# Block products in place of a plain channel product: seven instead of eight, in six of eight batches

## The chip, the cores and the metric

The kernel runs on one core of one Trainium2 chip. The metric is device time in microseconds from start to end of one execution. A core has five engines that run their own instruction queues in order: TensorE (PE in the profile, its weight loads PEld), VectorE (DVE), ScalarE (ACT), GpSimd (POOL) and SyncE (SP, which only issues DMAs here). They wait for one another by semaphores.

## What is computed

```python
# attention over 8 batches, 8 heads, 576 positions, head size 64
q_d, k_d, v_d = (t.reshape(B, H, S // 4, 4, D).mean(axis=3) for t in (q, k, v))
out_up = np.repeat(sm_attn(q_d, k_d, v_d), 4, axis=2)
mask = np.abs(pos[:, None] - pos[None, :]) < 4
out_local = softmax(where(mask, scale * q @ k.T, -1e9)) @ v
x = (out_up + out_local) laid out as (8, 576, 512)
# token mixing and channel mixing
h = relu(x.T @ w_tok1) @ w_tok2          # 576 -> 256 -> 576
u = x + h.T
out = u + relu(u @ w_ch1) @ w_ch2        # 512 -> 1536 -> 512
```

## The kernel before, in words

**Main products.** Per batch, `u` (512 channels by 576 positions, channels on partitions in four blocks c) is cut along the positions into chunk 0 (256 columns) and chunk 1 (320). A chunk goes through two *channel products*. The first (`first`, L720, matmuls `c<-uh,CW` recorded at L117) makes 12 blocks f of 128 hidden channels; the second (`second`, L744, matmuls `c<-h,CX`) makes four blocks of 128 outputs from the 12. Every factor is kept as an fp16 high part and an fp16 low part, and every product is three matmuls (`PASSES`: high by high, high by low, low by high). So each product of a chunk is 144 matmuls of 128 x 128 weights on 256 or 320 columns, and each has its own weight load.

In a batch they follow one another in four stages, named A, B, C and D from here on: **A** first product of chunk 0, **B** second product of chunk 0, **C** first product of chunk 1, **D** second product of chunk 1.

**What goes with them.** Before A and C the chunk's scale is found: a maximum per partition, a transpose and a broadcast by PE (`um_t`, `um_b`), three small DVE operations (L121 to L123). Then `scaled` (L640 on) makes `uh`: ACT writes the high part (L653), DVE the low part (L655), once per block c. After each block f, `first_up` takes the result out of PSUM: ACT the high part with the ReLU (L739), DVE the low part (L741). After each output block, `second_up` adds on DVE (L767) and SP sends it out. Three PSUM banks (`m`) serve these products in turn.

**Side work.** While batch b is in its channel products, the attention and the token mixing of batch b+1 are emitted between them: `pool_q` (sums `qd` of four positions, DVE L436 and L438), `pooled` (scores `sd`, softmax `pd`, transposes `td`, product `ad` on the shortened sequence), `local` (banded scores `sc` for five tiles of positions, softmax in a buffer `P`, transposes `pT`, product `av`, result `x`) and `mix` (splits `xh`, L584 and L586; products `t1` and `t2`). `ORDER` sets how the steps of `pooled` (p0 to p3) and `local` (l0 to l4) alternate. After each piece of main work `tick` emits side work until its estimated PE time has reached `SIDE * done / (FR * 24 * S)`: `FR` is the share of the batch's main work by which the side work is to be out. The `qk` tiles of batch b+2 are loaded when the last banded scores, `sc` of tile l4, have read those of b+1; `vr` loads pass through the `w` buffers and are summed on POOL (L414, L415).

For batch 0 and the beginning of batch 1 the order comes from a planner (`drive`). From batch 1 on the program is emitted in the loop at the end, and a scheduler then places each engine's instructions; what it chose is read from the order of the built program.

## Time and profile before

| | us |
|---|---|
| median of three runs | 952.71 |
| lowest and highest | 950.33, 953.01 |
| profiled execution, whole time | 951.0 |
| its span, first to last instruction | 949.2 |

The prediction shows the lines themselves. How to read them: a group row gives busy time, the mean duration of one instruction in ns, and the idle time in front; a timeline row gives start, length, engine, line, operation and how many instructions were merged; a windows row gives busy us and number of instructions of each engine in a stretch of time. Matmuls overlap in the array, so the length of one (217 ns and more) is not the distance between two: for a merged row of n matmuls the distance is (length of the row - length of one) / (n - 1).

### The profile page before, as it was taken

Reading aid. Unit: us, or ns where it says so; the run is one execution under the profiler, and the core shown is the slowest. Engines: PE = TensorE matmul, PEld = TensorE weight load, DVE = VectorE, ACT = ScalarE, POOL = GpSimd, SP = SyncE. Lnnn points to the kernel's source line nnn. Section 1 sums busy time; section 2 is a strip of 40 time slices with the busy share of each in tenths; the row PEclk is TensorE's granted clock in tenths of the full one; section 3 lists DMA queues with packets and bytes.
Section 4 is the critical chain, followed back from the end, with each engine's and each line's share of the span. In section 5 each row is a group of like instructions: output and inputs, shape, how many; then the busy total and the mean of one; then the engine's idle time right before and its main releaser. Section 6 shows DMA issues by size and latency. Waiting matters only on the chain.

```text
span 949.2 us, 25828 instructions
## 1 busy us (share of the span) xinstructions
PE 897.8 (95%) x11420; PEld 709.8 (75%) x11427; DVE 501.1 (53%) x1191; ACT 298.1 (31%) x627; POOL 137.6 (14%) x207
## 2 busy tenths in 40 slices
PE   8578799999989999999999999999999999999998
PEld 4345677777867788677987788777887878777876
DVE  7699998337552375526652275524653275324221
ACT  2356544214232141423323142422414142322120
POOL 6476420021120002100040002200021000000000
PEclk9879999999999999999999999999999999999999
DMA  9765420430170004400062002600052000000000
GB/s 236 232 230 172 132 70 15 147 91 27 45 191 15 21 10 135 114 8 22 2 202 46 16 15 84 166 8 22 3 183 65 15 16 13 27 1 28 13 12 28
DMA packets 28223, 68.31 MB, mean 72 GB/s; under 512 B 3504, under 2 KB 14000, under 8 KB 26864
## 3 DMA queue, kind: packets, MB, share of 16 engines
q1 hardware_dynamic: 25552, 64.30, 23.1%
q10 hardware_dynamic: 2560, 2.36, 0.9%
q8 instruction: 90, 1.47, 0.7%
q14 instruction: 21, 0.17, 0.1%
HBM read 54.85 MB, written 9.44 MB: 68 GB/s over the span
## 4 chain that ended last, share of the span: by engine, by line
PE 75%; DVE 12%; DMA 6%; ACT 3%; issue 3%; POOL 0%; SPq 0%; ACTq 0%; DVEq 0%; POOLq 0%
PE c L117 50%; PE t L117 10%; PE ad L477 3%; DMA qk<-in_qk_dram 3%; DMA vw<-od 3%; PE av L545 2%; PE sc L509 2%; PE t L609 2%; PE sd L450 2%; PE td L468 1%; PE pT L532 1%; DVE uh L655 1%; ACT x L550 1%; DVE pd L458 1%; PE busy L154 1%
## 5 line engine op out<-in xcount | busy, mean ns | idle before, releaser
L117 PE MATMUL c<-uh,CW 128*128 128x256 f16 (+1 forms) x2304 | 306.1, 287 | 3.7 <-DVE h L741 2.0
L117 PE MATMUL c<-h,CX 128*128 128x256 f16 (+1 forms) x2304 | 305.7, 287 | 0.0
L117 PEld LDWEIGHTS <-CW 128*128 128x128 f16 x2304 | 218.7, 98 | 70.6 <-issue 16.7
L117 PEld LDWEIGHTS <-CX 128*128 128x128 f16 x2304 | 218.5, 98 | 58.1 <-issue 1.6
L741 DVE SCALAR_TENSOR_TENSOR h<-c,h 128x256 f16<-128x256 f32 (+1 forms) x192 | 86.7, 452 | 133.5 <-ACT h L739 133.4
L739 ACT ACTIVATE h<-c 128x256 f16<-128x256 f32 (+1 forms) x192 | 77.8, 407 | 180.8 <-PE c L117 180.5
L414 POOL TENSOR_TENSOR vr<-vr 72x256 f32<-72x256 f32 x64 | 49.9, 783 | 491.1 <-DMA vr<-in_vr_dram 491.0
L767 DVE SCALAR_TENSOR_TENSOR u<-c,io,u 128x256 f32<-128x256 f32 (+1 forms) x64 | 32.9, 514 | 102.9 <-PE c L117 102.7
L117 PE MATMUL t<-xh,W 128*128 128x512 f32 x240 | 69.0, 421 | 5.3 <-DVE xh L586 4.0
L636 DVE TENSOR_REDUCE umx<-t 128x1 f32<-128x256 f32 (+1 forms) x64 | 29.2, 457 | 84.3 <-ACT u L634 75.4
L634 ACT COPY u<-t 128x256 f32<-128x256 f32 (+1 forms) x64 | 25.5, 398 | 136.7 <-PE t L117 110.8
L117 PE MATMUL t<-W,hid 128*128 128x256 f32 (+1 forms) x384 | 67.0, 308 | 0.1
L550 ACT COPY x<-av 128x512 f32<-128x512 f32 x32 | 18.7, 583 | 121.2 <-PE c L117 52.2
L117 PEld LDWEIGHTS t<-xh,W 128*128 128x128 f32 x240 | 43.6, 192 | 16.2 <-DVE xh L586 5.3
L117 PEld LDWEIGHTS t<-W,hid 128*128 128x128 f32 x384 | 53.3, 189 | 0.6 <-DVE C_n_m L558 0.3
L545 PE MATMUL av<-vw,pt 47*32 47x64 f32 x2304 | 33.8, 231 | 11.8 <-DMA vw<-od 5.9
L545 PEld LDWEIGHTS av<-vw,pt 47*32 47x32 f32 x2304 | 27.8, 109 | 19.6 <-DVE P L516 6.3
L477 PE MATMUL ad<-vd,ptd 72*72 72x65 f32 x512 | 38.7, 228 | 1.6 <-issue 1.1
L477 PEld LDWEIGHTS ad<-vd,ptd 72*72 72x72 f32 x512 | 37.0, 145 | 2.9 <-issue 2.3
L436 DVE TENSOR_REDUCE qd<-qk 128x72 f32<-128x288 f32 x64 | 25.9, 445 | 24.5 <-DMA qk<-in_qk_dram 24.4
L653 ACT ACTIVATE uh<-u,us 128x256 f16<-128x256 f32 (+1 forms) x64 | 29.5, 524 | 26.5 <-DVE us L123 19.3
L415 POOL TENSOR_TENSOR vd<-vr 72x128 f32<-72x128 f32 x64 | 34.6, 546 | 4.0
(114 smaller groups left out, 878.7 us busy)
## 6 DMA issues: line engine op xcount, KB each, us to landing
qk<-in_qk_dram SPq DMA_DIRECT2D x32, 579.0 KB
vw<-in_vw_dram SPq DMA_DIRECT2D x32, 351.0 KB
vr<-in_vr_dram SPq DMA_DIRECT2D x64, 144.0 KB
C_raw<-in_c_dram SPq DMA_DIRECT2D x16, 512.0 KB
out_dram<-u SPq DMA_DIRECT2D x32, 160.0 KB
C_raws<-in_c_dram SPq DMA_DIRECT2D x8, 512.0 KB
out_dram<-u SPq DMA_DIRECT2D x32, 128.0 KB
vw<-od ACTq DMA_DIRECT2D x32, 72.0 KB
```

What stands on the lines that cost most here:

```text
L117: nc.tensor.matmul(ps, lhs(a), rhs(c), start=first and i == 0, stop=last and i == 2, **kw)
L414: nc.gpsimd.tensor_add(t[:, 0:2], t[:, 0:2], t[:, 2:4])
L415: nc.gpsimd.tensor_add(st.vd[:, g, 2 * pr:2 * pr + 2, :D], t[:, 0].rearrange("p (h d) -> p h d", d=D), t[:, 1].rearrange("p (h d) -> p h d ...
L436: nc.vector.tensor_reduce(o, q[:, h], axis=AX.X, op=ALU.add)
L477: nc.tensor.matmul(ps[:, g, par], pt[:, par, kg, G * g:G * g + G], st.vd[:, kg, 2 * pr + par], start=kg == 0, stop=kg == 1)
L545: nc.tensor.matmul(ps[QB * j:QB * j + QB, par, D * hp:D * hp + D], pt[p, hp, QB * j:QB * j + QB], st.vw[h][p, g, D * hp:D * hp + D], start ...
L550: nc.scalar.copy(x[:n].rearrange("p hp two d -> p two hp d"), ps[:n, :, :4 * D].rearrange("p two (hp d) -> p two hp d", hp=4))
L636: nc.vector.tensor_reduce(umx[ch][:, c:c + 1], ps, axis=AX.X, op=ALU.max, apply_absolute_value=True)
L653: nc.scalar.activation(t[:, 0], st.u[ch][c], AF.Copy, scale=s)
L739: nc.scalar.activation(ht[:, 0], ps, AF.Relu)
L741: nc.vector.scalar_tensor_tensor(ht[:, 1], ps, 0.0, ht[:, 0], ALU.max, ALU.subtract)
L767: nc.vector.scalar_tensor_tensor(us[c], banks[c], io, us[c], ALU.mult, ALU.add)
```

## The change

From batch 2 on, the first channel product of a chunk is computed as one level of Strassen's scheme (in Winograd's form). The weights of a group of three pairs of blocks (f, f+2) are seen as 2 x 2 blocks A11, A12, A21, A22, and `u` as B11, B12, B21, B22: halves of the channels by halves of the chunk's columns. `seven` makes seven block products per group instead of eight, in two groups per chunk, each product 18 matmuls on 128 or 160 columns, in three PSUM banks X, Y and Z. Partial sums are copied to SBUF by ACT (`kept`) and added by DVE; the ReLU split (`put`) works on three blocks at once.

The sums of B blocks (T1 to T4) and the seven splits per chunk are made by `combined`, which is advanced between the pieces of the second product before. The sums of weight blocks S1 to S4 are made once, during batch 1 (`weight_sums`, `last_sums`), on DVE and POOL in turn, with ACT for the high parts.

To find room: `u` and `uh` in fewer and larger tiles, `x` in 4 buffers instead of 5, one tile for the last 64 positions instead of two, `w` in 3 slots instead of 4, and from batch 2 on two `P` buffers for the banded softmax instead of three. `ORDER` is changed in its last line: the scores of tile l4 come together with the product of l2 instead of l0. `FR` is 0.78 instead of 0.9.

```diff
-FR = 0.9
+FR = 0.78
...
 ORDER = """p0+p1 p0 p1 p0 p1 l0+l1 l0 l1 p0 p0 p1 p1 l0 l1 l0 l1 p0 p0 p1 p1 l0 l0 l1 l1
 p2+p3 p2 p3 p2 p3 l2+l3 l2 l3 p2 p2 p3 p3 l2 l3 l2 l3 p2 p2 p3 p3 p3
-l0+l4 l0 l4 l2 l2 l4 l4 l1+l2 l1 l2 l3 l3 l4 l4 l3+l4 l3 l4"""
+l0+l1 l0 l1 l2 l2 l3 l3 l2+l4 l2 l4 l4 l4 l4 l4 l3+l4 l3 l4"""
+FIRSTS = (0, 1, 4, 5, 8, 9)
+BY_GROUP = (0, 1, 4, 2, 3, 6, 5, 8, 9, 7, 10, 11)
...
-    BUFS = dict(cw=6, h=5, w=4, xh=3, x=5, u0=4, u1=8, uh0=4, uh1=4, qk=4, qd=1, vw=2, vd=1, pt=2, od=1, sm=12, ev=8, sc=24)
-
-    SLOTS = dict(gg=2, m=3, g=1, w=4)
+    BUFS = dict(cw=6, h=5, w=3, xh=3, x=4, u0=1, u1=2, uh=2, qk=4, qd=1, vw=2, vd=1, pt=2, od=1, sm=12, ev=8, sc=24,
+                S=7, f=3)
+
+    SLOTS = dict(gg=2, m=3, g=1, w=3)
...
-    PT = [sb.tile([128, H, 64], F32, name=f"P{i}") for i in range(3)]
+    PT = [T([128, H, 64], F32, "S", "P2") if i == 2 else sb.tile([128, H, 64], F32, name=f"P{i}") for i in range(3)]
...
-    x_last = [sb.tile([128, 4, 2, D], F32, name=f"x_last{i}") for i in range(2)]
-    for t in (W1[-1].bitcast(F32), *x_last):
...
-            tag = "w" if st.b > 1 else "x" if st.b or i < BUFS["x"] else "xh"
+            tag = "w" if st.b > 1 else "x" if st.b or i > 5 else "S"
...
-        early = {0: 8, 1: 5}.get(st.b, 0)
+        early = {0: 8, 1: 4}.get(st.b, 0)
...
-        pp = PT[(len(TILES) * b + t) % 3]
+        pp = PT[(len(TILES) * b + t) % 3 if b < 2 else t % 2]
...
-        x = st.x[t] = x_last[b % 2] if n == short else T([n, 4, 2, D], F32, "x", f"x{b}_{t}")
+        x = st.x[t] = x_last if n == short else T([n, 4, 2, D], F32, "x", f"x{b}_{t}")
...
-                    u = T([128, N], F32, f"u{ch}", f"u{b}_{ch}_{c}")
+                    if c == 0:
+                        st.u[ch] = T([128, 4, N], F32, f"u{ch}", f"u{b}_{ch}")
                     ps = banks[ch, c // 2][:, c % 2, :N]
-                    nc.scalar.copy(u, ps)
+                    nc.scalar.copy(st.u[ch][:, c], ps)
...
+        st.umx = umx
+        return [splits(), products(), takes()] + [scaled()] * (b < 2)
+
+    def scale_of(st, ch):
...
+        big = yield from everywhere(f"um{b}_{ch}", st.umx[ch])
+        inv = st.ui[ch] = T([128, 1], F32, "sc", f"ui{b}_{ch}")
+        s = T([128, 1], F32, "sc", f"us{b}_{ch}")
+        yield step("V", 0.45, give="g")
+        pow2(big, 2.0 ** -5, inv, s)
+        return s
...
+    def combined(st, ch):
+
+        b, n = st.b, CHUNKS[ch][1] // 2
+        s = yield from scale_of(st, ch)
+        u = st.u[ch]
+        b11, b12, b21, b22 = (u[:, 2 * i:2 * i + 2, n * j:n * j + n] for i in range(2) for j in range(2))
+        parts = st.uh[ch] = {}
+        tiles = [T([128, k, 2, 2, n], F16, "uh", f"uh{b}_{ch}_{k}") for k in (4, 3)]
...
+        def split(name, x):
+            k = len(parts)
+            t = parts[name] = tiles[k // 4][:, k % 4]
+            nc.scalar.activation(t[:, 0], x, AF.Copy, scale=s)
+            nc.vector.scalar_tensor_tensor(t[:, 1], x, s, t[:, 0], ALU.mult, ALU.subtract)
+
+        def less(x, y, name):
+            t = T([128, 2, n], F32, "f", f"{name}_{b}_{ch}")
+            nc.vector.tensor_sub(t, x, y)
+            return t
+
+        yield step("V", 1.0)
+        split("B11", b11)
+        split("B21", b21)
+        yield step("V", 1.0)
+        t1 = less(b12, b11, "T1")
+        split("T1", t1)
+        yield step("V", 1.0)
+        t2 = less(b22, t1, "T2")
+        split("T2", t2)
+        yield step("V", 1.0)
+        split("T3", less(b22, b12, "T3"))
+        yield step("V", 1.0)
+        split("T4", less(b21, t2, "T4"))
+        e = yield step("V", 1.0)
+        split("B22", b22)
+        make(("uh", b, ch), e)
...
+    SW = {}
+
+    def weight_sums():
+
+        tiles = [T([128, 2, 2, 256], F16, "S", f"SW{i}") for i in range(7)]
...
+        add, sub = ALU.add, ALU.subtract
+        for p, f in enumerate(FIRSTS):
+            a, a2 = C1.fin[f], C1.fin[f + 2]
...
+            for j in range(3):
+                SW[j + 1, p] = tiles[(3 * p + j) // 2][:, (3 * p + j) % 2]
+            eng = nc.vector if p % 2 else nc.gpsimd
+            s1 = total(eng, "S1", p, [(h21, add), (h22, add), (l21, add), (l22, add)])
+            put(eng, SW[1, p], s1)
+            yield
+            s2 = total(eng, "S2", p, [(s1, add), (h11, sub), (l11, sub)])
+            put(eng, SW[2, p], s2)
+            yield
+            s3 = total(eng, "S3", p, [(h11, add), (h21, sub), (l11, add), (l21, sub)])
+            put(eng, SW[3, p], s3)
+            yield
+
...
+    def last_sums():
+        for p, f in enumerate(FIRSTS):
+            a = C1.fin[f]
+            s2 = SW[2, p]
...
+            eng = nc.vector if p % 2 else nc.gpsimd
+            tc.keep_in_program_order(eng.tensor_tensor(t, a[:, 0, 256:], s2[:, 0], ALU.subtract))
+            eng.tensor_tensor(t, t, a[:, 1, 256:], ALU.add)
+            eng.tensor_tensor(t, t, s2[:, 1], ALU.subtract)
+            w = SW[4, p] = C1.fin[f + 2][:, :, :256]
+            nc.scalar.copy(w[:, 0], t)
+            eng.tensor_tensor(w[:, 1], t, w[:, 0], ALU.subtract)
+            yield
...
+    def seven(st, ch, tick, gap):
+
+        b, N = st.b, CHUNKS[ch][1]
+        n, uh = N // 2, st.uh[ch]
+        hs = st.h[ch] = {}
...
+        def product(ps, w, x, first_):
+            for i in range(3):
+                wt = weights(w, 3 * g + i)
+                for k in range(2):
+                    for j, (a, c) in enumerate(PASSES):
+                        nc.tensor.matmul(ps[:, i], wt[:, a, 128 * k:128 * k + 128], uh[x][:, c, k],
+                                         start=first_ and i == k == j == 0, stop=i == 2 and k == 1 and j == 2,
+                                         skip_group_check=True)
+
...
+        def kept(ps, name):
+            t = T([128, 3, n], F32, "f", f"{name}{b}_{ch}_{g}")
+            nc.scalar.copy(t, ps)
+            return t
...
+        def put(x, pack, j):
+            hi, lo = (pack[:, :, a, n * j:n * j + n] for a in range(2))
+            nc.scalar.activation(hi, x, AF.Relu)
+            nc.vector.scalar_tensor_tensor(lo, x, 0.0, hi, ALU.max, ALU.subtract)
+
+        for g in range(2):
+            packs = [T([128, 3, 2, NMAX], F16, "h", f"h{b}_{ch}_{g}_{i}") for i in range(2)]
+            for i in range(3):
+                f = FIRSTS[3 * g + i]
+                hs[f], hs[f + 2] = ((None, t[:, i, :, :N]) for t in packs)
+            X = bank(g, "mx")
+            product(X, "A11", "B11", True)
+            s = kept(X, "s")
+            tick()
+            Z = bank(1 - g, "mz")
+            product(Z, "A12", "B21", True)
+            nc.vector.tensor_add(s, Z, s)
+            put(s, packs[0], 0)
+            tick()
+            product(X, "S2", "T2", False)
+            u2 = kept(X, "v")
+            tick()
+            Y = bank(2, "my")
+            product(Y, "S1", "T1", True)
+            tick()
+            product(X, "S3", "T3", False)
+            u3 = kept(X, "y")
+            nc.vector.tensor_add(u3, Y, u3)
+            put(u3, packs[1], 1)
+            gap()
+            product(X, "A22", "T4", False)
+            put(X, packs[1], 0)
+            tick()
+            product(Y, "S4", "B22", False)
+            nc.vector.tensor_add(u2, Y, u2)
+            put(u2, packs[0], 1)
+            tick()
...
-                for f in range(4 * k, 4 * k + 4):
+                for i in range(4 * k, 4 * k + 4):
+                    f = BY_GROUP[i] if b > 1 else i
                     mm3(ps, lambda a: C2.fin[f][:, a, 128 * c:128 * c + 128], lambda a: st.h[ch][f][1][:, a],
-                        f == 0, f == NF - 1)
+                        i == 0, i == NF - 1)
...
+        def gap(n):
+            had = done[1]
+            tick(n)
+            while work.next is not None and done[1] < had + 0.6 and may(work.next):
+                done[1] += work.go()
...
         for ch in range(2):
...
-            g, u = Run(first(st, ch, ["h"] * 4)), Run(first_up(st, ch))
-            for _ in range(NF):
-                g.go()
-                u.go()
-                u.go()
-                tick(CHUNKS[ch][1])
+            if b > 1:
+                seven(st, ch, lambda: tick(6 * N / 7), lambda: gap(6 * N / 7))
+            else:
+                g, u = Run(first(st, ch, ["h"] * 4)), Run(first_up(st, ch))
+                for i in range(NF):
+                    g.go()
+                    u.go()
+                    u.go()
+                    tick(N)
+                    if ch:
+                        next(sums, None)
+            ahead_ = (b, 1) if ch == 0 else (b + 1, 0)
+            split = None
...
+                    if split is None and 1 < ahead_[0] < B and ("u", *ahead_) in made:
+                        split = combined(ready[ahead_[0]], ahead_[1])
+                    if split is not None:
+                        next(split, None)
+                    tick(N)
+                    if b == 1:
+                        next(late if ch else sums, None)
...
+            while 1 < ahead_[0] < B and ("uh", *ahead_) not in made:
+                if split is None:
+                    if ("u", *ahead_) in made:
+                        split = combined(ready[ahead_[0]], ahead_[1])
+                    else:
+                        work.go()
+                elif next(split, None) is None:
+                    break
```

What stands in each queue, for the beginning of stage C of batch 3 (names carry batch and chunk: `u3_0` is `u` of batch 3, chunk 0; side work has batch 4, its loads batch 5). DVE before, from the last output blocks of stage B on: `qd5` are the sums over the loads for batch 5, `r4_4` and `P0` belong to the softmax of tile l4, `h3_1_0` to the first blocks of stage C.

```order
L767 SCALAR_TENSOR_TENSOR u3_0_2_5804<-c2_3_0_2_6563,io3_0_6420,u3_0_2_5804 128x256
L436 TENSOR_REDUCE qd5_6939<-qk5_0_6901 128x72 x2
L438 TENSOR_REDUCE qd5_6939<-qk5_0_6901 128x144
L436 TENSOR_REDUCE qd5_6939<-qk5_1_6903 128x72 x2
L438 TENSOR_REDUCE qd5_6939<-qk5_1_6903 128x144
L436 TENSOR_REDUCE qd5_6939<-qk5_2_6905 128x72 x2
L438 TENSOR_REDUCE qd5_6939<-qk5_2_6905 128x144
L767 SCALAR_TENSOR_TENSOR u3_0_3_5851<-c2_3_0_3_6671,io3_0_6420,u3_0_3_5851 128x256
```

DVE after, from the same last output block on; `uh3_1` are the low parts of the seven splits, `xh4_0` the low part of the first split of the token mixing.

```order
L936 SCALAR_TENSOR_TENSOR u3_0_5961<-c2_3_0_3_7237,io3_0_6874,u3_0_5961 128x256
L683 SCALAR_TENSOR_TENSOR uh3_1_4_7126<-u3_1_6171,us3_1_7099,uh3_1_4_7126 128x320 x2
L683 SCALAR_TENSOR_TENSOR uh3_1_4_7126<-T1_3_1_7216,us3_1_7099,uh3_1_4_7126 128x320
L683 SCALAR_TENSOR_TENSOR uh3_1_4_7126<-T2_3_1_7250,us3_1_7099,uh3_1_4_7126 128x320
L519 TENSOR_TENSOR P0_108<-sc4_4_7169,mask2_72 64x2x4x38
L687 TENSOR_TENSOR T4_3_1_7335<-u3_1_6171,T2_3_1_7250 128x320
L523 TENSOR_REDUCE mx4_4_7223<-P0_108 64x8
L683 SCALAR_TENSOR_TENSOR uh3_1_3_7127<-T3_3_1_7317,us3_1_7099,uh3_1_3_7127 128x320
L524 TENSOR_TENSOR P0_108<-P0_108,mx4_4_7223 64x8x38
L683 SCALAR_TENSOR_TENSOR uh3_1_3_7127<-T4_3_1_7335,us3_1_7099,uh3_1_3_7127 128x320
L589 TENSOR_TENSOR xh4_0_7342<-x4_0_7100,xh4_0_7342 128x512
L529 TENSOR_REDUCE r4_4_7227<-P0_108 64x8
```

The splits of the chunk and the softmax of l4 stand here now, behind the last output block of B; the twelve `qd5` reductions follow them, between the `xh4` rows, where before nine of the twelve stood ahead of that output block. PE after, at the `t1` products of the token mixing in stage C (rows that only go on with the same product are left out at "..."):

```order
L859 MATMUL mz3_1_0_7395<-uh3_1_4_7126,CW0_134 128x160
L120 MATMUL t1_4_7359<-xh4_0_7342,W1_0_148 128x512
...
L120 MATMUL t1_4_7359<-xh4_0_7342,W1_0_148 128x512 x5
...
L535 MATMUL pT4_4_7231<-ident_61,P0_108 128x64 x4
...
L120 MATMUL t1_4_7359<-xh4_1_7417,W1_1_149 128x512
```

PE takes these between matmuls of the block products, so it waits there for whatever the `t1` rows need. ACT after, at the beginning of stage A: `s`, `v` and `y` are the copies out of bank X, `pd4` and `P` the exponentials of the side work.

```order
L869 COPY s3_0_0_6342<-mx3_0_0_6323 128x384
L464 ACTIVATE pd4_0_6378<-pd4_0_6378 72x576
L874 ACTIVATE h3_0_0_0_6321<-s3_0_0_6342 128x3x128
L464 ACTIVATE pd4_1_6382<-pd4_1_6382 72x576
L526 ACTIVATE P0_108<-P0_108 128x8x38
L869 COPY v3_0_0_6472<-mx3_0_0_6323 128x384
```

The copy `v` must be out of bank X before the third product may add to it, and it stands behind the exponential of the side work.

More of the change, by code (lines that the diff above doesn't have):

```diff
@@ L84, in tile_ups_attention_mixer @@
     nc.vector.memset(ones, 1.0)
[L86 removed]
+    junk = T([128, 512], BF16, "f", "junk")
     nc.vector.memset(junk, 1.0)
@@ new lines, in seven, with weights, bank @@
+    def seven(st, ch, tick, gap):
+        b, N = st.b, CHUNKS[ch][1]
+        n, uh = N // 2, st.uh[ch]
+        hs = st.h[ch] = {}
+        def weights(name, p):
+            f = FIRSTS[p]
+            if name[0] == "S":
+                return SW[int(name[1]), p]
+            w = C1.fin[f if name[1] == "1" else f + 2]
+            return w[:, :, :256] if name[2] == "1" else w[:, :, 256:]
+        def product(ps, w, x, first_):
[6 more added lines that the diff above has]
+                                         skip_group_check=True)
+        def bank(slot_, name):
+            now_in["m"] = (slot_ - 1) % SLOTS["m"]
+            return PM(f"{name}{b}_{ch}_{g}")[:, :3 * n].rearrange("p (i n) -> p i n", i=3)
+        def kept(ps, name):
+            t = T([128, 3, n], F32, "f", f"{name}{b}_{ch}_{g}")
+            nc.scalar.copy(t, ps)
+            return t
+        def put(x, pack, j):
[34 more added lines that the diff above has]
+            tick()
+        for f in range(NF):
+            make(("h", b, ch, f), now[0])
@@ L861, in tile_ups_attention_mixer @@
     work = Run(rest(left))
+    sums, late = weight_sums(), last_sums()
     for b in range(1, B):
```

50 lines of the change are left out of this document (29 added, 21 removed).

## Prediction

> **What bounds the kernel now.** I read the page first: the busy time of each engine, its share of the span and its instructions.
>
> ```profile
> PE 897.8 (95%) x11420; PEld 709.8 (75%) x11427; DVE 501.1 (53%) x1191; ACT 298.1 (31%) x627; POOL 137.6 (14%) x207
> ```
>
> TensorE is busy for 95% of the span; nothing else comes near. Next I cut one batch out of the middle and read the windows of its four stages A, B, C and D. The columns are: window, length, then busy time of PE, PEld, DVE, ACT and POOL, the granted clock, the DMA share and GB/s.
>
> ```profile
> 659.30:685.36 26.06, 25.31 (x491) 22.17 (x488) 18.38 (x46) 11.80 (x26) 0.00 (x0) 1.00 0.03 8
> 685.36:706.32 20.96, 20.96 (x299) 18.54 (x293) 12.05 (x31) 2.18 (x5) 5.83 (x11) 1.00 0.48 152
> 706.32:739.73 33.41, 32.72 (x428) 24.19 (x423) 14.52 (x30) 13.65 (x29) 5.24 (x6) 1.00 0.33 82
> 739.73:767.27 27.54, 27.46 (x205) 21.21 (x203) 8.67 (x28) 4.61 (x12) 0.00 (x0) 1.00 0.05 18
> sum 107.97, PE 106.45 PEld 86.11 DVE 53.62 ACT 32.24 POOL 11.07; mean PE 26.61 PEld 21.53 DVE 13.40 ACT 8.06 POOL 2.77
> ```
>
> Of 107.97 us PE is busy for 106.45, at full clock: it lacks 0.75 us in A, 0.69 in C, next to nothing in B and D. So shorter matmuls shorten the batch one for one, and any new wait of PE lengthens it one for one. DVE and ACT have room as a mean; the question is whether they have it in A and C, where DVE is already busy for 18.4 of 26 us and ACT for 13.7 of 33.
>
> **What the change takes away.** The last batch has no side work, so its timeline shows the bare products (start, length, count at the end). The fourth row is a burst of 128-column matmuls in the start-up, and the last two give one such matmul and the weight loads of the same kind of burst.
>
> ```profile
> 875.15 15.88 PE L117 MATMUL c<-uh,CW 128*128 128x256 f16 x144
> 906.59 19.72 PE L117 MATMUL c<-uh,CW 128*128 128x320 f16 x144
> 926.15 19.72 PE L117 MATMUL c<-h,CX 128*128 128x320 f16 x144
> 106.18 0.39 PE L326 MATMUL C_sum<-CX 128*128 128x128 bf16 x4
> L326 PE MATMUL C_sum<-CX x44: 217/218/234, 87.2 to 119.1; 128*128 128x128 bf16 x44
> 87.23 0.23 PEld L326 LDWEIGHTS <-CX 128*128 128x128 bf16 x4
> ```
>
> Between 875.15 and 906.59 lie 288 matmuls of 256 columns (144 of the first product, 144 of the second), (906.59 - 875.15)/288 = 109.2 ns apart; the 144 of 320 columns up to 926.15 are 19.56/144 = 135.8 ns apart: 0.416 ns per column. The burst of four (three distances and one length) gives (0.39 - 0.22)/3 = 57 ns at 128 columns, and the straight line through the two others gives 56. At 160 columns it is 57 + 32 x 0.416 = 70 ns. A chunk now takes 144 matmuls, after the change 2 groups x 7 products x 18 = 252. Per batch: before 144 x (0.1092 + 0.1358) = 35.3 us, after 252 x (0.057 + 0.070) = 32.0 us. The gain is 3.3 us a batch, **19.8 us** for six. (An eighth fewer products would be 4.4; the fixed part of each matmul eats the rest.)
>
> The Trainium skill has a rule against this, on the page "TensorE: Matmul & The Clock Gate", section "Back-to-back issue gap": in a sustained stream where each matmul has its own weight load, 128 columns cost about 81 ns each. By that, and 13 ns more at 160, a batch would need 252 x (81 + 94) ns = 44.1 us and lose 8.8. The burst above speaks against it (57 ns, with a load each), but it is only four long.
>
> **What it adds, and where that lies.** The rows of the operations that are the nearest to the new ones:
>
> ```profile
> L741 DVE SCALAR_TENSOR_TENSOR h<-c,h 128x320 f16<-128x320 f32 x96 | 46.6, 485 | 84.9 <-ACT h L739 84.8
> L741 DVE SCALAR_TENSOR_TENSOR h<-c,h 128x256 f16<-128x256 f32 x96 | 40.2, 419 | 48.6 <-ACT h L739 48.6
> L634 ACT COPY u<-t 128x320 f32<-128x320 f32 x32 | 13.6, 425 | 77.2 <-PE t L117 67.5 <-DVE umx L636 9.6
> L634 ACT COPY u<-t 128x256 f32<-128x256 f32 x32 | 11.9, 371 | 59.6 <-PE t L117 43.3 <-DVE umx L636 16.3
> ```
>
> From 256 to 320 columns DVE takes 66 ns more and ACT 54, so three blocks of 128 (384 columns) are about 0.55 us on DVE and 0.48 on ACT, three of 160 about 0.65 and 0.56: estimates along these lines. Per batch DVE makes 14 such adds and splits for each chunk, 14 x (0.55 + 0.65) = 16.8, in place of 12 x (0.419 + 0.485) = 10.8; three more splits and four subtractions for each chunk, 7 x (0.42 + 0.48), are 6.3 more. That is about 12 us on top of 53.6. As a mean, 66 of 105 us, it is nothing. ACT gains about 8 on 32. So what counts is the order in the queues, and there I walked stages C and A through, row by row.
>
> **Stage C.** Rows of DVE around the beginning of C before, then of PE:
>
> ```profile
> 698.33 0.47 DVE L516 TENSOR_TENSOR P<-sc,mask 64x304 f32<-64x304 f32 x1 [1.00 <-PE sc L509]
> 698.83 0.46 DVE L520 TENSOR_REDUCE mx<-P 64x8 f32<-64x304 f32 x1
> 699.32 0.78 DVE L521 TENSOR_TENSOR P<-P,mx 64x304 f32<-64x304 f32 x1
> 703.67 0.81 DVE L436 TENSOR_REDUCE qd<-qk 128x72 f32<-128x288 f32 x2 [2.24 <-DMA qk<-in_qk_dram]
> 705.11 0.81 DVE L436 TENSOR_REDUCE qd<-qk 128x72 f32<-128x288 f32 x2
> 711.73 0.46 DVE L526 TENSOR_REDUCE r<-P 64x8 f32<-64x312 f32 x1
> 712.51 0.18 DVE L527 RECIPROCAL r<-r 64x8 f32<-64x8 f32 x1
> 712.97 0.46 DVE L528 TENSOR_TENSOR P<-P,r 64x304 f32<-64x304 f32 x1
> 713.36 2.15 DVE L586 TENSOR_TENSOR xh<-x,xh 128x512 fp32r<-128x512 f32 x3
> ```
>
> ```profile
> 697.71 0.48 PE L509 MATMUL sc<-qk 64*32 64x38 f32 x32
> 700.75 0.60 PE L532 MATMUL pT<-ident,P 128*128 128x128 f32 x4
> 711.08 1.58 PE L545 MATMUL av<-vw,pt 47*32 47x64 f32 x128
> 716.15 1.66 PE L117 MATMUL t<-xh,W 128*128 128x512 f32 x6 [0.23 <-ACT x L550]
> ```
>
> ```profile
> L117 PE MATMUL t<-xh,W 128*128 128x512 f32 x240 | 69.0, 421 | 5.3 <-DVE xh L586 4.0 <-ACT x L550 1.2
> ```
>
> Before, the softmax of tile l4 begins at 698 and the sums `qd` run from 703.67, most of them while B's matmuls still cover them; the splits `uh` of C are made in A. After the change one DVE row waits for B's last output block, and behind it stand, ahead of the low part of the third `xh` for which `t1` on PE waits: that row, about 0.5; seven splits of 320 columns at 0.48 (the L741 row), 3.4; T4, about 0.5; the softmax of l4, 0.47 + 0.46 + 0.78 + 0.46 + 0.18 + 0.46 = 2.8; four times the `qd` sums of a tile, 705.11 - 703.67 = 1.44 each, 5.8; an add and a split of 480 columns, 1.3; three `xh`, 2.15. Together 16.4 to 16.5 us. In the same stretch PE has: the scores `sc` 0.4, four `pT` 0.45, `av` of two tiles 1.5, 91 matmuls of the block products at 70 ns 6.4, `pT` and `av` of l4 0.7, 13 rows of `t1` at (1.66 - 0.42)/5 = 0.25, 3.3. Together 12.7. PE waits for the difference, about 3.8 us, where it lacked 0.7: **+3.1 us a batch**. Ends: 0 if the scheduler's places for the `qd` rows come out earlier in time than they stand here, 6 if the loads land late as well (the row at 703.67 waited for one) and hold the whole queue behind them.
>
> **Stage A.** Here the scores `sc` must wait until DVE has read the scores `sd` in the same banks, and `sd` now stands behind seven splits.
>
> ```profile
> 655.04 0.38 PE L567 MATMUL um_b<-um_m,ones 1*128 1x1 f32 x2
> 660.70 1.21 PE L450 MATMUL sd<-qd 64*72 64x144 f32 x16
> 664.39 0.77 PE L509 MATMUL sc<-qk 64*32 64x38 f32 x64 [0.74 <-issue]
> 656.64 1.28 DVE L655 SCALAR_TENSOR_TENSOR uh<-u,us,uh 128x256 f16<-128x256 f32 x3 [0.64 <-ACT uh L653]
> 662.15 1.41 DVE L456 TENSOR_REDUCE mxd<-sd 72x4 f32<-72x576 f32 x2
> 663.48 1.17 DVE L458 TENSOR_TENSOR pd<-sd,mxd 72x288 f32<-72x288 f32 x3
> L523 ACT ACTIVATE P<-P 128x304 f32<-128x304 f32 x32 | 14.6, 457 | 30.5 <-DVE P L521 30.5
> ```
>
> Counted from `um_b` on PE: 24 matmuls of D 3.3, two `sd` 1.2, two products of 18 at 57 ns 2.05, so `sc` is due at 6.5. On DVE: 0.4 for `um_b`, 1.2 from its end to the first split (655.42 to 656.64), seven splits at 1.28/3 = 0.43, T4 0.4, D's last `u` 0.5, `mxd` 0.7, two `pd` 0.9: 7.1, so PE waits 0.6. The second `sc` is due 0.9 later and needs `mxd`, `pd`, the add of 384 columns and `pd`, 2.15: PE waits 1.25 more. Then PE has 1.7 (the rest of that stretch and a product) plus 0.9 before the third product may add to bank X, and ACT's copy `v` stands behind the exponential `P` (0.46), which stands behind five DVE rows of 0.46 to 0.55: 2.4 + 0.46 + 0.48 = 3.4, so 0.8. Together 2.65, with a tenth at the copies of the second group 2.75, where A lacked 0.75 before: **+2.0 us a batch**. Ends: 0, and 4 if each group pays all of it.
>
> **The last batch.** The next product in bank X waits for the copy `y`: the end of the matmul after its issue, 0.16, the copy at 0.48 or 0.56, and the handing over, say 0.1, together 0.75. In the other batches `gap` puts 0.6 us of side work there; the last has none. Four groups: **+3.0 us**. (Copies `s` and `v` have a product of 1.0 to 1.3 us over them.)
>
> **Batch 1.** The weight sums are made among its work: 24 tensors, 45 operations on DVE at 0.43 us (the 256-column row above), 19 us, as many on POOL at
>
> ```profile
> L414 POOL TENSOR_TENSOR vr<-vr 72x256 f32<-72x256 f32 x64 | 49.9, 783 | 491.1 <-DMA vr<-in_vr_dram 491.0
> 218.59:330.89 112.30, 109.43 (x1408) 86.89 (x1407) 54.74 (x136) 33.66 (x74) 12.06 (x21) 0.98 0.23 62
> ```
>
> 0.78, 35 us, and 24 copies on ACT. The window of batch 1 has DVE busy for 55 and POOL for 12 of 112 us, so the sums fit, but they stand between rows for which PE waits. PE lacks 2.9 us there now; I take it that this doubles, **+3 us**. Ends: 0; 8, if half of DVE's 19 is felt. The smaller pools I cost at nothing: POOL, which sums the loads that pass through three `w` slots, is busy for a tenth of a batch. If that cover is gone, it is a microsecond or two in all, within the ends above.
>
> **The sum.** The profiled execution took 951.0 us, 1.7 under the median of 952.71 and inside the three runs. A and C carry side work in five of the six batches (2 to 6; after batch 7 none follows): 951.0 - 19.8 + 5 x (3.1 + 2.0) + 3.0 + 3 = 962.7. The forecast is **963 us**, 1% slower.
>
> **Rivals.**
> 1. *DVE keeps ahead* (faster). What decides is the wait per batch in A and C. At no more than now the time is 951.0 - 19.8 + 3 + 3 = 937; at a quarter of my 5.1 it is 944: 941. The point where it turns is 19.8 - 6 = 13.8 us over five batches, 2.8 a batch. For it: DVE is idle for half of the time, and side work is emitted earlier (`FR`), which moves some DVE rows out of C's end. Against: the walk, where DVE is short by 3 to 4 us in one stretch. Chance 0.31.
> 2. *No net change*: waits of about half my sum, 951.0 - 19.8 + 13 + 6 = 950, 948 to 954. Chance 0.12.
> 3. *Weight loads set the pace.* A load of this kernel takes about as long as the matmul it precedes is apart:
>
> ```profile
> L117 PEld LDWEIGHTS <-CW 128*128 128x128 f16 x2304 | 218.7, 98 | 70.6 <-issue 16.7
> ```
>
> If loads could not overlap, 504 x 0.098 = 49.4 us would stand for 35.3, and DVE's delays would vanish under them: 951 + 6 x 14.1 + 6 = 1042. Against it, four loads in 0.23 us (87.23 above): if one is 98 ns long, they are (0.23 - 0.10)/3 = 44 ns apart. By the 81 ns of the Trainium skill's page it would be 951 + 6 x 8.8 + 6 = 1010. Chance for either 0.05.
>
> **The numbers.** The forecast, slower by over 0.3%, has 0.52, with its own range from 955 (waits of 3.5 a batch) to 980 (8 a batch: 951.0 - 19.8 + 40 + 6 = 977, and batch 1 at its upper end). 0.3% is about what a measurement of this kernel tells from no change. Faster then has 0.31, the same 0.12, slower 0.52 + 0.05 = 0.57. The range must reach to rival 1 as well; from 938 to 980 it leaves out the best of rival 1 (0.08), rival 3 (0.05) and the tail above (0.06).
>
> **What would show it right or wrong.** Right: 128-column matmuls 56 to 58 ns apart and 160-column ones 69 to 71 in bare stretches; in stage C the first `t1` rows, or the block product just ahead, wait 3 to 5 us a batch with DVE `xh` or `uh` as the releaser; in A `sc` and the third product wait, released by DVE `pd` and ACT `v`; in the last batch four gaps of about 0.75 behind `y`. Wrong: PE busy to within 2 us of each batch's length (then rival 1), or distances above 65 and 78 ns (then rival 3); waits on DMA `qk` ahead of the DVE rows in C would mean that the queue is held by the loads and not by its own work.

## The result and the profile after

| | before | after |
|---|---|---|
| median of the runs (6 each) | 952.86 us | 958.64 us |
| lowest and highest | 950.33, 954.93 | 955.1, 962.06 |
| ratio, 95% interval | | 1.006 [1.0032, 1.0088] |
| profiled execution | 951.0 us | 960.02 us |

The change makes the kernel slower by 5.8 us, 0.6%. The page of the kernel after, busy time by engine; TensorE does 1,296 matmuls more and is busy a little less, DVE and ACT have 79 and 51 us more:

```profile
PE 896.9 (94%) x12716; PEld 740.6 (77%) x12723; DVE 579.9 (61%) x1344; ACT 349.4 (36%) x711; POOL 165.5 (17%) x251
```

A batch in the middle, batch 4, by its stages A to D (same columns as in the prediction: length, then PE, PEld, DVE, ACT, POOL, clock, DMA share, GB/s):

```profile
560.02:584.69 24.67, 23.87 (x589) 22.28 (x590) 19.50 (x47) 11.55 (x23) 0.00 (x0) 1.00 0.03 11
584.69:608.28 23.59, 23.59 (x430) 20.73 (x427) 9.87 (x30) 5.97 (x12) 9.37 (x17) 1.00 0.32 87
608.28:644.04 35.76, 34.13 (x440) 30.05 (x433) 25.40 (x52) 17.08 (x35) 0.00 (x0) 1.00 0.36 108
644.04:667.92 23.88, 23.34 (x176) 17.08 (x174) 8.72 (x24) 4.92 (x12) 0.00 (x0) 1.00 0.06 21
sum 107.90, PE 104.93 PEld 90.14 DVE 63.48 ACT 39.52 POOL 9.37; mean PE 26.23 PEld 22.53 DVE 15.87 ACT 9.88 POOL 2.34
```

107.90 us, where the batch of before that the prediction shows (batch 5) had 107.97: this batch has gained nothing. `FR` has moved side work out of D (27.5 to 23.9 us) into B and C. PE is idle for 2.97 us instead of 1.52: in C 1.63 (before 0.69), in A 0.80 (0.75), and in D 0.54 (0.08), which is one wait just ahead of the next A.

The bare distances of the short matmuls, 18 in a row at 128 columns (in the last batch) and at 160:

```profile
885.69 1.17 PE L859 MATMUL mx<-uh,CW 128*128 128x128 f16 x18
620.64 1.41 PE L859 MATMUL mx<-uh,SW 128*128 128x160 f16 x18
```

With one length of 0.22 and 0.23 us, (1.17 - 0.22)/17 = 56 ns and (1.41 - 0.23)/17 = 69 ns. The two first products of a batch need 252 x (0.056 + 0.069) = 31.5 us of PE, 3.8 less than before. The gain is there; something takes it back.

Where, by stretches of the span. First before, batch 1 and then batches 2 to 6 together:

```profile
218.59:330.89 112.30, 109.43 (x1408) 86.89 (x1407) 54.74 (x136) 33.66 (x74) 12.06 (x21) 0.98 0.23 62
330.89:875.15 544.26, 533.39 (x7024) 430.68 (x7022) 266.45 (x665) 164.04 (x356) 43.39 (x68) 1.00 0.18 52
```

and after:

```profile
221.73:339.61 117.88, 111.69 (x1406) 87.47 (x1405) 74.16 (x184) 41.54 (x98) 47.27 (x66) 0.97 0.19 58
339.61:884.88 545.27, 527.04 (x8102) 453.27 (x8100) 314.79 (x751) 200.08 (x406) 37.33 (x68) 0.99 0.17 52
```

Up to batch 1 the profiled executions differ by 3.1 us (221.73 against 218.59), in batch 1 by 5.6, in batches 2 to 6 by 1.0, in the last batch by -0.7 (74.05 against 73.32): 9.0, their whole difference. The first term is no effect of the change that could be shown: in the profiles of the kernels below, batch 1 begins anywhere between 217.2 and 223.2 us, in one whose source differs from the changed kernel's only behind that point at 217.3.

Batch by batch, in us; ownput is a kernel of the experiments whose source differs from the changed kernel's only in batch 1, room one without block products:

| batch | 2 | 3 | 4 | 5 | 6 | sum |
|---|---|---|---|---|---|---|
| before | 111.32 | 107.89 | 109.20 | 107.97 | 107.88 | 544.26 |
| room | 109.82 | 109.51 | 109.47 | 108.55 | 107.98 | 545.33 |
| after | 112.13 | 108.28 | 107.90 | 111.57 | 105.39 | 545.27 |
| ownput | 111.07 | 107.91 | 107.90 | 108.83 | 105.40 | 541.11 |

Batches 4 and 6 repeat in the last two rows, batches 2 and 5 do not: so the sum of one profile is good to some 4 us, and a difference of 1.0 tells no more than that little is gained or lost. Batch 6 has gained 2.5. Its side work, for the last batch, has no loads and no `qd` sums. Its D is 1.35 us shorter than in batch 4, with eight `sd` matmuls (0.65 us) and the wait ahead of the next A missing; its C is 1.17 shorter.

What PE waits for in batch 4 of after (total, times, longest):

```profile
PE mx L859 <- DVE u L936: 1.1, 2, 0.5
PE av L548 <- ACT x L553: 0.6, 1, 0.6
PE t L120 <- ACT x L553: 0.6, 1, 0.6
PE sc L512 <- DVE pd L461: 0.4, 2, 0.2
PE t L120 <- DVE xh L589: 0.4, 1, 0.4
PE mx L859 <- ACT y L869: 0.2, 1, 0.2
PE t L120 <- ACT hid L624: 0.2, 1, 0.2
```

and in batch 5 of before:

```profile
PE sc L509 <- issue: 0.7, 1, 0.7
PE pT L532 <- ACT pt L536: 0.3, 1, 0.3
PE t L117 <- ACT x L550: 0.2, 1, 0.2
```

Two waits for `u` are listed: one of 0.53 us, which ends where the window begins, and one of 0.54 at its end. With the second alone PE waits for 3.0 us against 1.2, in eight places instead of three, none over 0.6. The rest of the 3.8 does not stand in this view, which counts a matmul's own length of 0.2 us as busy: a wait behind a short matmul is longer by 0.16 (0.23 - 0.07) than the view says. That this makes up the whole rest is not shown.

### The profile page after: what moved, and what is told of

It is laid out like the page before. It is cut to its first block, busy times and chain, and to the rows that moved or that the text cites. A ratio compares the mean times of both kernels' runs of the same rounds, so it can differ in the third digit from the quotient of the medians.

```text
span 958.2 us, 28701 instructions
## 1 busy us (share of the span) xinstructions
PE 896.9 (94%) x12716; PEld 740.6 (77%) x12723; DVE 579.9 (61%) x1344; ACT 349.4 (36%) x711; POOL 165.5 (17%) x251
## 4 chain that ended last, share of the span: by engine, by line
PE 69%; DVE 17%; ACT 5%; issue 4%; POOL 3%; DMA 2%; ACTq 0%; DVEq 0%; POOLq 0%
PE c L120 29%; PE t L120 10%; PE mx L859 9%; PE my L859 5%; PE ad L480 3%; PE mz L859 2%; PE av L548 2%; PE pT L535 2%; DVE pd L461 2%; PE t L612 2%; DVE uh L683 1%; PE td L471 1%; PE sc L512 1%; DVE mxd L459 1%; DMA vw<-od 1%
## 5 line engine op out<-in xcount | busy, mean ns | idle before, releaser
L120 PE MATMUL c<-h,CX 128*128 128x256 f16 (+1 forms) x2304 | 300.7, 287 | 0.2 <-ACT h L874 0.2
L859 PEld LDWEIGHTS <-CW 128*128 128x128 f16 x1872 | 120.4, 99 | 16.3 <-issue 9.9
L120 PE MATMUL c<-uh,CW 128*128 128x256 f16 (+1 forms) x576 | 81.3, 292 | 2.0 <-DVE h L787 2.0
L120 PE MATMUL t<-xh,W 128*128 128x512 f32 x240 | 73.4, 435 | 6.6 <-DVE xh L589 4.8
L859 PE MATMUL mx<-uh,CW 128*128 128x128 f16 (+1 forms) x936 | 71.7, 228 | 5.4 <-DVE u L936 2.1
L120 PE MATMUL t<-W,hid 128*128 128x256 f32 (+1 forms) x384 | 69.5, 311 | 1.3 <-ACT hid L624 1.0
L120 PEld LDWEIGHTS <-CW 128*128 128x128 f16 x576 | 54.9, 100 | 19.9 <-issue 5.8
L859 PEld LDWEIGHTS <-SW 128*128 128x128 f16 x1008 | 64.2, 98 | 5.8 <-issue 3.8
L859 PE MATMUL mx<-uh,SW 128*128 128x160 f16 (+1 forms) x648 | 50.1, 226 | 0.3
L682 ACT ACTIVATE uh<-u,us 128x256 f16<-128x256 f32 (+1 forms) x36 | 17.9, 530 | 69.4 <-DVE io L935 62.1
```

The source lines that it names most:

```text
L120: nc.tensor.matmul(ps, lhs(a), rhs(c), start=first and i == 0, stop=last and i == 2, **kw)
L859: nc.tensor.matmul(ps[:, i], wt[:, a, 128 * k:128 * k + 128], uh[x][:, c, k], start=first_ and i == k == j == 0, stop=i == 2 and k == 1 an ...
```

## The experiments

All ratios are to the kernel before, which ran beside each group. The theory at first was that of the prediction: rows of DVE pile up at the beginning of A and C. The rivals were that making room or moving steps costs, that the weight sums cost, and that the waits are many and small.

**What goes with the change, without the block products (room).** The plain product in all batches, with neither weight sums nor sums of blocks of `u`:

```diff
-            if b > 1:
+            if b > 99:
                 seven(...)
-        return [splits(), products(), takes()] + [scaled()] * (b < 2)
+        return [splits(), products(), takes()] + [scaled()]
```

> All that the change does beside the block products: the smaller pools, two P buffers, the new last line of ORDER and FR = 0.78, but the plain product in all batches and no weight sums. Theory (the loss comes from DVE work of the block products that piles up in stages C and A): nothing of that work is here, so this is within 2 us of the kernel before, ratio 0.998 to 1.003, and steady batches of 107 to 109 us. Rival (the room-making or the moved steps are what costs, and the block products themselves gain their 20 us): ratio 1.02 to 1.03.

957.5 us, 1.0036 [1.0012, 1.0061]; between the two. A steady batch and its two longest waits:

```profile
550.60:660.07 109.47, 107.38 (x1407) 86.16 (x1405) 53.12 (x133) 32.74 (x70) 9.31 (x17) 1.00 0.20 61
```

```profile
PE pT L535 <- DVE P L531: 1.3, 1, 1.3
PE sc L512 <- DVE pd L461: 0.6, 1, 0.6
```

Between the batches shown, making room and moving side work costs 1.5 us (107.97 to 109.47) before any block product is made, and the block products then gain 1.6. Neither holds for all five batches: the table above has 545.33 us for room, 1.1 more than before in all, since before has two longer batches of its own and batch 6 is the same in both. The median of room is 4.8 us above that of before, its profiled execution (952.46 us) only 1.5, so where the rest lies is not shown.

**The weight sums left out (nosums).**

```diff
+            SW[1, p], SW[2, p], SW[3, p] = a2[:, :, :256], a2[:, :, 256:], a[:, :, 256:]
...
+            SW[4, p] = a[:, :, 256:]
```

(in place of the sums, so that the block products read plain weight blocks)

> The changed kernel without the 24 sums of weight blocks (the block products read plain weight blocks in their place). Theory: batch 1, 5.6 us longer than before in the profile, falls back to 112 to 113 us; the whole is 3 to 6 us under the changed kernel, ratio to before 1.000 to 1.003. Rival (batch 1 is longer because of the smaller pools and the other FR): no change, ratio 1.005 to 1.007.

950.0 us, 0.9961 [0.9938, 0.9985], 8.6 us under the changed kernel, more than either side expected. Batch 1:

```profile
221.66:330.62 108.96, 107.89 (x1407) 86.05 (x1405) 54.01 (x139) 34.02 (x74) 11.60 (x21) 1.00 0.22 62
```

The sums cost 117.88 - 108.96 = 8.9 us there, and without them batch 1 is even shorter than before. Up to 3.4 of the 8.9 are clock: with the sums, C of batch 1 has two windows of 3.4 us at half clock (last section), without them batch 1 has none. It is the only kernel of the series below the kernel before, and it is not a whole one: the price of the sums decides whether the change gains or loses.

**The old ORDER with two P buffers (oldorder).**

```diff
-l0+l1 l0 l1 l2 l2 l3 l3 l2+l4 l2 l4 l4 l4 l4 l4 l3+l4 l3 l4"""
+l0+l4 l0 l4 l2 l2 l4 l4 l1+l2 l1 l2 l3 l3 l4 l4 l3+l4 l3 l4"""
```

> The changed kernel with the old last line of ORDER: the scores of tile l4 come with the product of l0 again, so the softmax of l4 (2.8 us of DVE) leaves the pile at the beginning of stage C, and the loads for the next batch start earlier. Theory (the pile in C decides): stage C of a steady batch is 1.5 to 2.8 us shorter, the whole 7 to 14 us, ratio to before 0.991 to 0.999. Rival (the waits in C come from ACT, or the pile only moves to stage B): within 2 us of the changed kernel, ratio 1.004 to 1.008.

975.2 us, 1.0223 [1.0191, 1.0256]. A badly built experiment: in this order the softmax of l4 is written into the P buffer before l2's transposes have read it. Both use buffer 0 of the two, so l2's product is made of l4's values. PE's longest wait in batch 2 is 3.4 us for a DMA ahead of the product `av`. The run says nothing on the pile, only why two P buffers need another order.

**Half of each qd sum (lightqd).**

```diff
-            nc.vector.tensor_reduce(o, q[:, h], axis=AX.X, op=ALU.add)
+            nc.vector.tensor_reduce(o, q[:, h][..., :2] if st.b > 2 else q[:, h], axis=AX.X, op=ALU.add)
```

(and `k` likewise)

> The changed kernel with the sums over four positions (qd) reduced to sums over two from batch 3 on: 24 rows as before, but each over half the elements, some 2.5 us of DVE less in the pile of stage C. Theory: 1 to 2.5 us a batch over four to five batches, 4 to 12 us in all, ratio to before 0.994 to 1.002. Rival (DVE's pile is covered, ACT or the order on PE sets the wait): ratio 1.004 to 1.008.

961.95 us, 1.0087 [1.0058, 1.0116]; stage C is 35.64 us long, where it was 35.76. No gain: the rival's answer.

**Two splits instead of seven (twosplits).**

```diff
-        t1 = less(b12, b11, "T1")
-        split("T1", t1)
...
+        for name in ("T1", "T2", "T3", "T4", "B22"):
+            parts[name] = parts["B21"]
```

> The changed kernel without the four sums of B blocks and with two of the seven splits per chunk: the products that read T1 to T4 and B22 read the split of B21 in their place. PE's order and count stay; DVE has some 4.3 us less per chunk and ACT 2.6, all of it at the beginning of A and C. Theory (this pile makes the waits of A and C): 2 to 4 us a batch, 12 to 22 us in all, ratio to before 0.983 to 0.994. Rival (the waits come from the copies out of the banks and from the handing over to side work): within 4 us of the changed kernel, ratio 1.002 to 1.008.

961.13 us, 1.0093 [1.0062, 1.0124]: no gain either, though DVE has 6.8 us less in the batch (56.73 instead of 63.48). DVE's timeline shows what now holds its queue at the beginning of C, and the waits of PE for the batch:

```profile
613.82 0.45 DVE L439 TENSOR_REDUCE qd<-qk 128x72 f32<-128x288 f32 x1 [0.43 <-DMA qk<-in_qk_dram]
614.62 0.46 DVE L531 TENSOR_TENSOR P<-P,r 64x304 f32<-64x304 f32 x1
616.55 0.45 DVE L439 TENSOR_REDUCE qd<-qk 128x72 f32<-128x288 f32 x1 [0.82 <-DMA qk<-in_qk_dram]
620.76 1.28 DVE L589 TENSOR_TENSOR xh<-x,xh 128x512 fp32r<-128x512 f32 x2
```

```profile
PE t L120 <- DVE xh L589: 1.3, 1, 1.3
PE pT L535 <- DVE P L531: 1.2, 1, 1.2
```

The wait for `u` ahead of A (0.53) is gone, so the splits did make that one. But DVE now stands idle before `qd` rows whose loads have not landed, with the last softmax row and `xh` behind them, and PE waits longer for these than before. The loads were issued from 606.80 on in the changed kernel, 1.5 us before C began, and in the kernel before (batch 5) from 698.36 on, 8 us before C began, since they follow the scores of l4, which ORDER has moved.

**No qd sums at all (noqd).**

```diff
+        if st.b > 2:
+            st.qd = ready[st.b - 1].qd
+            make(("q", st.b, hp), e)
+            return
```

> The changed kernel without the sums qd from batch 3 on (the scores of the shortened sequence read those of batch 2): twelve DVE rows a batch fewer, and with them DVE's waits for the loads qk, which in the trace of twosplits held the queue of stage C once it was lighter. Theory as it stands now (in C PE waits for rows behind these twelve, and either their own time or the late loads keep them there, so that taking out one of the two alone shows nothing): C 2 to 3 us shorter in batches 2 to 5, 8 to 14 us in all, ratio to before 0.991 to 0.998. Rival (many small waits at the hand-overs, none of them bound to these rows): ratio 1.004 to 1.008.

955.89 us, 1.0047 [1.0019, 1.0075]. The batch is 107.29 us, its C this:

```profile
608.13:643.28 35.15, 33.82 (x441) 29.80 (x433) 20.01 (x40) 17.20 (x35) 0.00 (x0) 1.00 0.38 112
```

With the `qd` rows and their waits for loads both out of DVE's queue, C gains 0.6 us of the 2 to 3 expected. The theory falls in this form too; the other waits (ACT `x` twice, `u`, `sc`) stay where they were. The loads themselves still run here; no run took them out.

**The scores of l4 one step earlier (midl4).**

```diff
-l0+l1 l0 l1 l2 l2 l3 l3 l2+l4 l2 l4 l4 l4 l4 l4 l3+l4 l3 l4"""
+l0 l0 l2 l2 l1+l4 l1 l4 l3 l3 l4 l4 l2 l2 l4 l4 l3+l4 l3 l4"""
```

> The changed kernel with the scores of tile l4 taken earlier by one step (with the product of l1 instead of l2), the earliest that two P buffers allow. Theory (the softmax of l4 in the pile of C costs PE time): stage C 1 to 2 us shorter, 5 to 10 us in all, ratio to before 0.995 to 1.001. Rival (its place does not matter, since the reductions that follow it may be taken out without effect): ratio 1.004 to 1.008.

961.59 us, 1.0103 [1.007, 1.0137]. C falls by the expected 1.5 us to 34.23, and D rises by 1.2, from 23.88 to 25.10:

```profile
613.11:647.34 34.23, 33.01 (x426) 28.68 (x423) 24.41 (x51) 16.19 (x33) 0.00 (x0) 1.00 0.37 106
647.34:672.44 25.10, 24.57 (x185) 18.23 (x183) 9.56 (x25) 5.32 (x12) 0.00 (x0) 1.00 0.06 20
```

The batch as a whole (107.83) is as long as in the changed kernel: side work that leaves a stage comes back in another, and a shorter stage alone proves nothing. Batch 1, which follows the same ORDER, takes 123.03 us here, 5.2 more than in the changed kernel; batches 2 to 6 take 539.79, 5.5 less, nearly all of it in batches 2 and 5, which vary between profiles. So the median says little on the place of l4 in a steady batch.

**room with the old ORDER and three P buffers (roomorder).**

```diff
-        pp = PT[(len(TILES) * b + t) % 3 if b < 2 else t % 2]
+        pp = PT[(len(TILES) * b + t) % 3]
```

> The room kernel (no block products) with the old last line of ORDER and three P buffers again; pools and FR as after the change. Theory (in room, the one wait of PE for the late softmax of l4, 1.5 us a batch in its trace, is the price of ORDER and the two P buffers): 1.5 us a batch off room over six batches, ratio to before 0.993 to 1.000. Rival (the pools or FR cost room its time): as room, 1.002 to 1.006.

958.76 us, 1.0079 [1.0049, 1.0108]. The wait for the late softmax is gone (0.2 left), and PE waits for the product's operand instead, a DMA that comes late (batch 3):

```profile
PE av L548 <- DMA vw<-od: 1.7, 2, 1.5
PE av L548 <- issue: 0.9, 1, 0.9
```

So the old ORDER with three buffers does not win the time back; `FR`, which packs the attention tighter, and the pools remain as causes, untested in this kernel.

**FR = 0.9 in the changed kernel (fr90).**

```diff
-FR = 0.78
+FR = 0.9
```

> The changed kernel with FR = 0.9 as before the change: side work is spread into stage D again. Theory of density (room, without block products, is 1.5 us a batch longer than before, and roomorder, with the old ORDER, is too, so it is FR that packs the side work of A to C so tightly that PE meets its latencies): 1 to 2.5 us a batch, 6 to 14 us in all, ratio to before 0.992 to 1.000. Rival (the pile of block-product work on DVE in A and C): no gain, ratio 1.004 to 1.010.

977.56 us, 1.0251 [1.0217, 1.0284], a clear loss. A steady batch of it is 109.84 us long, and PE waits in it for `sc` (1.9) and `pT` (0.9). Batch 1 takes 126.44 us, 8.6 more than in the changed kernel, and batches 2 to 6 take 552.70, 7.4 more. The density theory falls for this kernel: spread out, the side work costs more, and about half of that in batch 1, beside the sums.

**The high parts of the sums by the summing engine (ownput); the sums in B and D only (bd).** The changed kernel's timelines in batch 1 show the case for the first: ACT waits 2.13 us for a sum of POOL, and the copy `x` behind it is what PE waits 2.43 us for:

```profile
280.98 0.41 ACT L806 CAST SW<-S 128x256 f16<-128x256 f32 x1 [2.13 <-POOL S L801]
281.29 0.58 ACT L553 COPY x<-av 128x512 f32<-128x512 f32 x1
281.92 0.86 PE L548 MATMUL av<-vw,pt 47*32 47x64 f32 x64 [2.43 <-ACT x L553]
```

```diff
-            nc.scalar.copy(t[:, 0], x)
+            eng.tensor_copy(t[:, 0], x)
```

> The changed kernel with the high part of each weight sum made by the engine that made the sum (DVE or POOL) instead of by ACT. Theory (ACT's queue stands in batch 1 behind copies that wait for POOL, and with it the copies x and h for which PE waits): 4 to 7 us off batch 1, ratio to before 0.999 to 1.002. Rival (the DVE operations themselves, or POOL's use of SBUF beside DVE, cost the time): no gain, or a loss of up to 3 us by 12 more operations on DVE, ratio 1.005 to 1.010.

```diff
-                    if ch:
-                        next(sums, None)
...
-                        next(late if ch else sums, None)
+                        next(sums, None)
```

> The changed kernel with the weight sums made in stages B and D of batch 1 alone (12 and 12), none during stage C. Theory (what costs in batch 1 is that ACT stands in C behind copies that wait for sums, and x behind them: its C is 43 us in the changed kernel, 37 without the sums): C back to 37 to 39 us, 4 to 6 us in all, ratio to before 0.999 to 1.002. Rival (the sums cost the same wherever they are, and in D they delay batch 2): ratio 1.004 to 1.008.

958.01 us, 1.0058 [1.0038, 1.0078], and 960.55 us, 1.0079 [1.0047, 1.011]. Batch 1 is 119.82 and 119.33 us, no shorter. In the first, the waits for ACT are gone, but DVE, with more rows, is now what PE waits for:

```profile
PE pT L535 <- DVE P L531: 3.5, 1, 3.5
PE t L120 <- DVE hid L626: 2.4, 1, 2.4
```

In the second, C is still 41.4 us (43.0 in the changed kernel), and A of batch 2 begins with a wait of 1.5 us for a split of ACT, as the rival had it: the scheduler places the rows by its own view, and writing the sums in other stages did not keep them out of C.

**All sums on POOL (poolsums).**

```diff
-            eng = nc.vector if p % 2 else nc.gpsimd
+            eng = nc.gpsimd
```

(with the high parts on POOL as well)

> The changed kernel with all 24 weight sums made on POOL alone, high parts too: some 114 operations of about 0.75 us, 85 us beside 12 of its own in a batch of 112, and no row of the sums on DVE or ACT. Theory (the sums cost their 9 us because their rows on DVE and ACT stand ahead of rows for which PE waits): batch 1 back to 109 to 113 us, 5 to 9 us in all, ratio to before 0.997 to 1.001. Rival (POOL beside DVE slows both, or is too late for the first block products of batch 2): stage A of batch 2 longer by what is missing, ratio 1.006 to 1.020.

973.35 us, 1.0219 [1.019, 1.0248]; batch 1 takes 130.49 us. Neither theory had the way it goes: it is not batch 2 that is late. The sums of the loads `vr` stand behind the weight sums on POOL, the `w` slots stay full, and SP's queue stands for 22 us at the next `vr` load, with the loads `qk` behind it; DVE waits for those, and behind that row PE's transposes (8.65 us). ACT's copy `x` stands for 26.10 us behind the same `vr` loads, and PE waits another 8.88 us for it:

```profile
257.35 22.34 SPq L403 DMA_DIRECT2D vr<-in_vr_dram  x5
293.06 1.88 SPq L388 DMA_DIRECT2D qk<-in_qk_dram  x4
298.41 0.81 DVE L439 TENSOR_REDUCE qd<-qk 128x72 f32<-128x288 f32 x2 [8.43 <-DMA qk<-in_qk_dram]
301.21 0.69 PE L535 MATMUL pT<-ident,P 64*128 64x64 f32 x4 [8.65 <-DVE P L531]
```

## Why the prediction came out right, and which of its terms did not

The forecast was 963 us, slower, with 938 to 980; measured are 958.64, slower. By its own steps:

- **The gain** of 3.3 us a batch was right, slightly low: 57 and 70 ns were assumed, 56 and 69 found, 3.8 us. The figure of the Trainium skill's page "TensorE: Matmul & The Clock Gate", section "Back-to-back issue gap", 81 ns for 128 columns in a stream with a weight load each, does not hold here; the trace has 56 over 18 in a row. Rival 3 is out.
- **The waits of A and C**, 5.1 us a batch, were too large, and the cause of those in C failed. The batches 2 to 6 were to grow by 5 x (5.1 - 3.3) = 9; they grew by 1.0, and in ownput's profile they were 3.2 shorter than before. With a gain of 3.8 that is 3.2 to 4.0 taken back a batch; in the changed kernel's profile up to 0.7 of it by two half-clock windows (below).
  In A the waits taken as 0.6, 1.25 and 0.8 came out as 0.1, 0.4 and 0.2, by the starts of PE's rows. PE came to them later than was counted: it had waited 0.6 for `u` just ahead of A, a wait that the sum did not have.
  In C the step that failed is "PE waits for the difference" of DVE's work and its own. PE in the walked stretch of batch 4, up to the first row for the third `xh`:

```profile
609.50 0.86 PE L548 MATMUL av<-vw,pt 47*32 47x64 f32 x64 [0.56 <-ACT x L553]
611.86 0.49 PE L120 MATMUL t<-xh,W 128*128 128x512 f32 x1 [0.56 <-ACT x L553]
618.73 1.65 PE L120 MATMUL t<-xh,W 128*128 128x512 f32 x6 [0.35 <-DVE xh L589]
622.08 2.80 PE L120 MATMUL t<-xh,W 128*128 128x512 f32 x11
```

  DVE had the third `xh` ready 15.5 us after its row for B's last output block, where 16.5 were walked. But PE needed 15.6 us itself (606.47 to 622.08) for what was counted as 12.7. It lost 2.9 on the way, not 3.8 at the end: twice behind ACT's copy `x`, once behind the second `xh`, the rest in small amounts. In noqd the third `xh` is ready after 8.6 us, and PE still needs about 15 for the same rows. With 2.3 to 6.8 us of DVE work taken out of a batch, in three ways, C did not shorten by more than 0.6. So the difference of two sums is not what PE waits for: it waits at hand-overs to ACT and DVE ahead of the row that the walk looked at.
- **The last batch**: predicted 3.0 of gaps against 3.3 of gain, measured a gain of 0.73. In the gap behind `y`, taken as 0.75 us, PE does half a product of the next group; what is left is 0.28, and other small waits take the rest. This is the row, its 27 matmuls being 9 of the next group's product and 18 of this one's:

```profile
890.32 1.95 PE L859 MATMUL mx<-uh,CW 128*128 128x128 f16 x27
```

- **Batch 1**: predicted 3, measured 5.6, and 8.9 by taking the sums out. The step that failed was that the sums fit beside other work because DVE is busy for half of the time: in-order queues made ACT, DVE and SP each wait for a sum or behind one, whichever engine had it; and the clock, which no term of the sum had, makes up to 3.4 of the 8.9 (two windows at half clock, where before has one).
- **The total.** The sum of 962.7 came out close to the profiled 960.0 by errors of both signs: batches 2 to 6 were 8.0 too high, batch 1 was 2.6 too low, the last batch 0.4 too high and the start-up 3.1 too low. That they so nearly cancel is luck.
- **Not in the sum**: the clock windows below, and the start-up's scatter of up to 6 us between the profiles.

Of the signs, the distances came as said; the waits in A and C came smaller than said, in C mostly from ACT; waits of DVE for `qk` in C did not come in the changed kernel, only in twosplits. Rival 1 asked for waits under 2.8 us a batch and PE idle for less than 2; 3.2 to 4.0 were taken back, and PE is idle for 2.97. Rival 2, no net change, is what batches 2 to 6 show alone.

What stays open is what holds the steady batch at 107.3 to 107.9 us in lightqd, midl4, noqd and the changed kernel. Shown is that leaving out five of DVE's splits, leaving out its `qd` sums and moving l4, one at a time, do not shorten it by more than 0.6. In stage C the step from 35.76 us to 35.15 without `qd` sums goes on to 34.59 in batch 6, which has no loads either, so the loads may have a part. That many short hand-overs between block products and side work do the rest is argued, not shown. Which of `FR` and the pools makes room's batches 3 and 4 longer than 107.9 was not separated.

## What to carry to other kernels

Fewer multiplications that need more additions trade time of the bound engine for rows in the in-order queues of the others; the means of those (61% busy at most here) say little about it. Price one-time preparation as carefully as the steady state: here 24 small sums cost the gain of more than two batches, and in none of the three other placements was batch 1 shorter. Compare all batches of two kernels, not one of each: here two batches of five differ by up to 2.7 us between two profiles whose source is the same there. And test a theory of a queue by emptying that queue: three kernels with a lighter DVE refuted a sum that gave nearly the right total.
